# Attention into a mixture of experts on one core: the spread of the input scale gets a buffer of its own width, and the second layer's halves, sums and readings follow a new table of steps

## The chip, the core and the metric

The program runs on one core of one Trainium2 chip. The core has four compute engines, each with an instruction queue that it works off in order: TensorE (PE, matrix products into the accumulators called PSUM), VectorE (DVE), ScalarE (ACT) and GpSimd (POOL). Almost all transfers between the chip's main memory and the core's working memory are issued by a fifth queue, SyncE (SP). An instruction waits at the head of its queue for semaphores that others raise. The metric is the device time of one execution in microseconds (us), from the first to the last instruction plus a small margin, as the median of several runs.

## The reference, cut to what matters

Attention over clusters gives x, 3,072 rows of 512. Then comes a dense mixture of 8 experts: every expert works on every row, and a gate that is normalised eight times in both directions weighs the results.

```python
h = np.maximum(x @ w1[e], 0.0)        # 3072x512 @ 512x1024, for e in range(8)
ye = h @ w2[e]                        # 3072x1024 @ 1024x512
out += P[:, e:e + 1] * ye
```

All of it is float32. The kernel gets that precision out of 16-bit products: each operand is split into a "hi" half (the value rounded to 16 bits) and a "lo" half (what the rounding left), and three products hi·hi, hi·lo, lo·hi are summed.

## The kernel before, in words

**Stages.** The 3,072 rows are four batches b of 768. The first stage is the attention for all batches; each batch of x is stored to main memory (`xd`). The second stage does both layers of all eight experts for batch 0 and prepares the first-layer weights for the rest: 32 blocks t (eight experts, four quarters f2 of the 1,024 hidden columns each). The third stage does batches 1 to 3: 24 slots n, one for each pair (b, e) of batch and expert.

**Seven products instead of eight.** Both layers use Strassen's scheme on 2 by 2 blocks, in the variant with running sums: sums and differences of blocks (S1 to S4 of the left operand, T1 to T4 of the right) are formed first, and seven products replace eight. In the third stage a slot is cut into 28 steps (`SLOT`). In each step the program emits one of the 28 first-layer products of slot n (`layer1b`, seven m = 0..6 for each of the four f2; six matmuls at L1125 each) and a quarter of one of the seven second-layer products of slot n-1 (`layer2b`, nine matmuls at L1532). So the second layer of a slot runs one slot later than its first layer. In the planner's tables, `base` is the first step of the slot in which a slot's second layer runs.

**What feeds the second layer.** The first layer's results are the blocks B11, B12, B21, B22 of each of two row groups g (g = 0 from f2 = 0 and 1, g = 1 from f2 = 2 and 3). POOL forms the differences T1 to T4 of these (`minus`, L1433). Then ACT writes the hi half of each operand (`high`, L1438), and DVE the lo half (`low`, L1442), into tiles called `ho`. The product of operand i of the list ORDER2 (B11, T1, T2, B21, T3, B22, T4) takes the steps base+4i to base+4i+3: two for g = 0, two for g = 1. At the end of each product DVE adds it, weighed by the gate, to the running results (`evict`, L1508): six instructions for the first product, three for each later one. The left operands `w2o` are loaded eight steps ahead (`load_left`, L1446) into three buffers.

**What the first layer needs of the other engines.** A PSUM tile of layer 1 is read by ACT (L1148, L1571) or by DVE's "add" (L1139) before PE may use that buffer again; there are two buffers, so the product m = 6 waits for the add of m = 4.

**The second layer's weights.** In the eight slots of batch 1 the S blocks of the second matrix are made as well, one f2 after the other: SP loads a block into `r` (L1450, two buffers of pool `rp`), POOL forms four sums in `s2w` (`second_sums`, four instructions at L1181, one buffer of pool `sp`), ACT and DVE make their halves `w2s` (`second_high` L1459, `second_low` L1463), and SP stores them to `w2d` (L1466), from which `load_left` reads.

**The next batch's input.** `next_x` (L1089) is a generator that is stepped once in a block of the second stage and four times in a slot of the third. It loads x of the next batch in four blocks, takes the largest absolute value of each, forms differences (`less`, on POOL, L301), and writes the halves of seven operands. In between stands `spread_powers` (L1065). It finds the largest value over all 128 partitions: `am` (one number for each partition) is stored to a small tile in main memory (`amx`, L1068) and read back so that every partition gets all 128 numbers (`all`, L1070). The same function serves the weights with n = 2 numbers a partition (`amw`). Its tile is 128 by 2 numbers wide whatever n is, so that for n = 1 every second number of a row is filled.

**Who sets the order.** In the second and third stage each engine's order is the order in which the program is written: `at(time, ...)` files a small task under a step, and at each step the program emits the layer-1 product, the leftovers of the step before, the tasks of this step, a step of `next_x` (at every seventh), and the layer-2 quarter. So a row of `plan_slot` (L1471) decides where in an engine's queue an instruction stands. SP's queue is in the same order: a load that has to wait holds back the loads behind it.

Of the kernel before, what the change touches and what calls it, by code (L numbers as in the profile page):

```python
# [8 lines left out]
F32 = mybir.dt.float32  # L9
# [5 lines left out]
ALU = mybir.AluOpType  # L15
AX = mybir.AxisListType.X
# [4 lines left out]
P = 128  # L21
# [135 lines left out]
def attn_moe_kernel(  # L157
# [11 lines left out]
    nc = tc.nc  # L169
# [35 lines left out]
    first = const.tile([2, 1], F32, name="first")  # L205
# [62 lines left out]
    def input_use(b, g, pool):  # L268

        nc.vector.tensor_copy(gx[:, b : b + 1], g)  # L270
        inv = pool.tile([P, 1], F32, name="xinv")
        nc.vector.tensor_scalar(out=inv, in0=g, scalar1=1.0 / MX, scalar2=None, op0=ALU.mult)
        nc.vector.reciprocal(sx[:, b : b + 1], inv)
# [16 lines left out]
    def largest(out_, in_):  # L290
        nc.vector.tensor_reduce(out=out_, in_=in_, axis=AX, op=ALU.max, apply_absolute_value=True)
# [7 lines left out]
    def less(o, a, c, by=nc.vector):  # L299
        t = tmp.tile([P, KC, HB], F32, name="tx")  # L300
        by.tensor_tensor(out=t, in0=xq[a], in1=xq[c], op=ALU.subtract)  # L301
        xq[o] = t

    def split_hi(b, o):
        nc.scalar.activation(xs[b][o][:, 0], xq[o], AF.Copy, scale=sx[:, b : b + 1])

    def split_lo(b, o):
        nc.vector.scalar_tensor_tensor(
            out=xs[b][o][:, 1].rearrange("p c s -> p (c s)"), in0=xq[o].rearrange("p c s -> p (c s)"), scalar=sx[:, b : b + 1],
            in1=xs[b][o][:, 0].rearrange("p c s -> p (c s)"), op0=ALU.mult, op1=ALU.subtract,  # L310
        )

    with ExitStack() as actx:
# [48 lines left out]
        bufs = {nm: [] for nm in NSET}  # L362
# [644 lines left out]
    NP2 = NF // 2  # L1007
# [8 lines left out]
    def pool(name, bufs, under=ctx, **kw):  # L1016
        return under.enter_context(tc.tile_pool(name=name, bufs=bufs, reuse_waits="tile", **kw))
# [8 lines left out]
    gs = pool("gs", 2)  # L1026
# [38 lines left out]
    def spread_powers(am, n, name, use):  # L1065

        d = dram.tile([P, n], F32, name=name)
        nc.sync.dma_start(out=d, in_=am)  # L1068
        t = gs.tile([P, P, 2], F32, name="all")
        nc.sync.dma_start(out=t[:, :, 0:n], in_=d.partition_broadcast(P))  # L1070
        yield
        yield
        yield
        g = gs.tile([P, 2], F32, name="gmax2")
        nc.vector.tensor_reduce(out=g[:, 0:n], in_=t[:, :, 0:n].rearrange("p q n -> p n q"), axis=AX, op=ALU.max)
        nc.vector.tensor_scalar(out=g[:, 0:n], in0=g[:, 0:n], scalar1=float(2.0**-100), scalar2=None, op0=ALU.max)
        nc.vector.tensor_single_scalar(out=g[:, 0:n].bitcast(I32), in_=g[:, 0:n].bitcast(I32), scalar=0x7F800000, op=ALU.bitwise_and)
        use(g[:, 0:n])
        yield
# [9 lines left out]
    def next_x(b):  # L1089

        am4 = gs.tile([P, 4], F32, name="am4")
        for i, o in enumerate(XQ):
            k, j = divmod(i, 2)
            xq[o] = pers.tile([P, KC, HB], F32, name=f"xq{o}", tag=xq_from[o][1])
            nc.sync.dma_start(out=xq[o], in_=xd[b][:, k * KC : (k + 1) * KC, j * HB : (j + 1) * HB])
        yield
        for i, o in enumerate(XQ):
            largest(am4[:, i : i + 1], xq[o].rearrange("p c s -> p (c s)"))
            yield
        for t, a, c in LESS["T2"]:  # L1100
            less(t, a, c, nc.gpsimd)
        am = gs.tile([P, 1], F32, name="am")
        nc.vector.tensor_reduce(out=am, in_=am4, axis=AX, op=ALU.max)
        yield from spread_powers(am, 1, f"amx{b}", lambda g: input_use(b, g, gs))
        yield
        for o in XS:
            if o == "B21":
                for t, a, c in LESS[o]:
                    less(t, a, c, nc.gpsimd)
            xs[b][o] = xp.tile([P, 2, KC, HB], F16, name="xst")  # L1110
            split_hi(b, o)
            split_lo(b, o)
            nc.sync.dma_start(out=xsd[b][o], in_=xs[b][o].rearrange("p x c s -> p (x c s)"))
            yield
# [80 lines left out]
    with ExitStack() as ax:  # L1195
# [17 lines left out]
        def scan(idx):  # L1213

            e, f2 = divmod(idx, NP2)
            if f2 == 0:
                ams[e] = gs.tile([P, 2, NP2], F32, name="am8")
            for m in range(2):
                largest(ams[e][:, m, f2 : f2 + 1], raws[idx][:, m * 1024 : (m + 1) * 1024])
                yield  # L1220
            if f2 == NP2 - 1:
                am2 = gs.tile([P, 2], F32, name="am2")
                nc.vector.tensor_reduce(out=am2, in_=ams[e], axis=AX, op=ALU.max)
                yield from spread_powers(am2, 2, f"amw{e}", lambda g: weight_use(e, g, gs))
# [113 lines left out]
        for t in range(NI):  # L1338
            e, f2 = divmod(t, NP2)
# [11 lines left out]
            if t == 8:  # L1351
                inputs = next_x(1)
# [57 lines left out]
        plan.keep_order()  # L1410

    rp = pool("rp", 2)
    sp = pool("sp", 1)
    w2p = pool("w2p", 2)
    hbp = pool("hbp", 3)
    hop = pool("hop", 6)
# [5 lines left out]
    SLOT = 7 * NP2  # L1422
    tasks = {}

    def at(time, f, *a):
        tasks.setdefault(time, []).append((f, a))
# [44 lines left out]
    def plan_slot(n):  # L1471

        b, e = slots[n]
        base = SLOT * (n + 1)
        for g, (t1, t2, t3, t4), off in ((0, (-4, -3, -2, 8), -6), (1, (1, 2, 3, 11), -3)):
            at(base + t1, minus, n, g, "T1", "B12", "B11", "B11")
            at(base + t2, minus, n, g, "T2", "B22", "T1", None)
            at(base + t3, minus, n, g, "T3", "B22", "B12", "B12")
            at(base + t4, minus, n, g, "T4", "B21", "T2", "B21")
            for i, (_, o) in enumerate(ORDER2):  # L1480
                late = 1 if g and o == "T1" else 0
                at(base + 4 * i + off + late, high, n, g, o)
                at(base + 4 * i + off + late + 1, low, n, g, o)
        for i in range(7):
            at(base + 4 * i - 8, load_left, n, i)
        at(base - 1, gate_slot, n)
        if b == 1:
            for f2 in range(NP2):
                t0 = base - SLOT + 6 * f2
                at(max(t0 - 4, 0), load_second, e, f2)  # L1490
                at(t0 + 1, second_sums, e, f2)
                at(t0 + 3, second_high, e, f2)
                at(t0 + 4, second_low, e, f2)

    CHAINS = ("pa", "pc", "pb", "pa", "pb", "pc", "pb")
    INTO = ((("C21", 0), ("X", 1)), (("C22", 1),), (("C12", 1),), (("C11", 0),), (("C22", 1),), (("C12", 1),), (("C21", 0),))
# [83 lines left out]
    for n in range(NS):  # L1580
        plan_slot(n)
    inputs = iter(())
    for n in range(NS + 1):
        one = layer1b(n) if n < NS else iter(())
        two = layer2b(n - 1) if n else iter(())
        if n < NS:
            b, e = slots[n]
            if e == 1 and b + 1 < B:
                inputs = next_x(b + 1)
        for s in range(SLOT):  # L1590
            now = SLOT * n + s
            old = rests[:]
            rests.clear()
            step(one)
            for f in old:
                f()
            for f, a in tasks.pop(now, ()):
                f(*a)
            if s % 7 == 5:
                step(inputs)  # L1600
            step(two)
            plan.keep_order()
# [24 lines left out]
```

## Time and profile before

| | us |
|---|---|
| median of 3 runs | 2664.49 |
| the runs | 2663.87, 2664.49, 2674.68 |
| the profiled execution, its own time | 2661.44 |
| its span, first to last instruction | 2659.7 |
| PE busy in the span | 2305.4 (87%) |
| DVE, ACT, POOL busy | 1711.6, 1038.4, 1097.9 |
| mean granted TensorE clock | 0.937 |

The profile is of one execution. In its timelines a row gives start, length, engine, line, operation, what is written and read, how many such in a row, and in brackets how long the engine was idle just before and who ended that wait. "SPq" is SP issuing a transfer: its length is how long the issue held the queue, not how long the transfer took. In the chain of waits (the work that ended last, followed back) a row is start, length and what. A block of the second stage takes 14.60 us when nothing is in the way, a slot of the third 55.27 us, and so a step of a slot 1.97 us.

### The profile page before, as it was taken

The numbers are of one execution on the slowest core, as the hardware profiler recorded it, in microseconds if no ns is written. First come the engines' busy times: TensorE is split into PE (matmuls) and PEld (weight loads), VectorE is DVE, ScalarE is ACT, GpSimd is POOL, SyncE is SP. The second block draws the span as 40 slices with busy tenths as digits, with TensorE's granted clock in tenths as the row PEclk, the third lists the DMA queues.
The fourth block names the chain that finished last, engine by engine and source line by source line (L and its number), as shares of the span: only waits on it lengthen the run. The fifth ranks groups of instructions, "written<-read, shape, count | busy, mean of one in ns | idle before, by whom it ended". The sixth has DMA issues, their size and how long they took to land.

```text
span 2659.7 us, 39413 instructions
## 1 busy us (share of the span) xinstructions
PE 2305.4 (87%) x15410; PEld 1529.2 (57%) x15410; DVE 1711.6 (64%) x2834; ACT 1038.4 (39%) x1849; POOL 1097.9 (41%) x1007
## 2 busy tenths in 40 slices
PE   7999999879961999899069999992499999999998
PEld 4565565435530545467047777771377777777777
DVE  7888888687841776477047776661266656666667
ACT  4565555534430444343024444331143333333333
POOL 5676777535440455254045455230132233223223
PEclk7999999889985999999579999996799999999999
DMA  7444655264613552574156656530354354444343
GB/s 150 105 117 92 146 130 140 69 227 145 196 31 87 167 169 97 182 260 143 1 185 221 218 198 230 189 120 1 103 164 151 127 175 157 141 133 133 128 134 95
DMA packets 261740, 376.14 MB, mean 141 GB/s; under 512 B 114864, under 2 KB 190768, under 8 KB 261040
## 3 DMA queue, kind: packets, MB, share of 16 engines
q1 hardware_dynamic: 261552, 373.61, 46.1%
q8 instruction: 121, 1.98, 0.3%
q14 instruction: 67, 0.55, 0.1%
HBM read 265.27 MB, written 79.57 MB: 130 GB/s over the span
## 4 chain that ended last, share of the span: by engine, by line
PE 71%; DVE 12%; SPq 6%; another core or an unknown queue 3%; DMA 3%; POOL 2%; issue 2%; ACT 1%; DVEq 0%; ACTq 0%; POOLq 0%
PE h_ps L1125 29%; PE pb L1532 10%; PE pa L1532 6%; PE pc L1532 5%; SPq L1086 5%; PE av_ps L825 4%; PE o_ps L1305 3%; PE o_ps L1304 3%; PE o_ps L1306 3%; PE max_ps L698 2%; PE exp_ps L766 2%; DVE ho L1442 2%; PE exp_ps L767 2%; DVE mrt L702 2%
## 5 line engine op out<-in xcount | busy, mean ns | idle before, releaser
L1125 PEld LDWEIGHTS <-wa 128*128 128x128 f16 x5376 | 529.2, 99 | 454.6 <-issue 157.4
L1532 PEld LDWEIGHTS <-ho 128*128 128x128 f16 x6048 | 593.5, 98 | 309.2 <-issue 169.3
L1125 PE MATMUL h_ps<-xsT,wa 128*128 128x384 f16 x3072 | 591.3, 329 | 103.5 <-DVE u L1139 78.5
L1532 PE MATMUL pb<-w2o,ho 128*128 128x256 f16 x2592 | 331.4, 274 | 167.6 <-DMA w2o<-w2d 167.1
L1125 PE MATMUL h_ps<-xsB,wa 128*128 128x384 f16 x2304 | 440.7, 328 | 35.0 <-DVE B L1139 33.0
L1433 POOL TENSOR_TENSOR B<-B,B 128x768 f32<-128x768 f32 x96 | 181.4, 1890 | 602.4 <-DVE ho L1442 417.1
L1573 ACT ACTIVATE B<-B 128x384 f32<-128x384 f32 x288 | 149.6, 520 | 516.9 <-DVE B L1139 516.9
L1139 DVE SCALAR_TENSOR_TENSOR u<-h_ps,m 128x384 f32<-128x384 f32 x256 | 141.6, 553 | 325.6 <-PE h_ps L1125 322.5
L1442 DVE TENSOR_TENSOR ho<-B,ho 128x768 f16<-128x768 f32 x288 | 326.1, 1138 | 14.2 <-ACT ho L1438 14.2
L792 POOL TENSOR_TENSOR psum<-psum,pe 128x512 f32<-128x512 f32 (+1 forms) x203 | 221.8, 1110 | 46.1 <-ACT pe L773 40.3
L1438 ACT CAST ho<-B 128x768 f16<-128x768 f32 x288 | 231.6, 824 | 12.4 <-POOL B L1433 7.2
L1532 PE MATMUL pc<-w2o,ho 128*128 128x256 f16 x1728 | 220.5, 274 | 1.3 <-DVE ho L1442 1.3
L1532 PE MATMUL pa<-w2o,ho 128*128 128x256 f16 x1728 | 219.0, 273 | 0.0
L702 DVE TENSOR_REDUCE mrt<-max_ps 128x1 f32<-128x512 f32 (+1 forms) x288 | 189.9, 683 | 38.4 <-PE max_ps L698 36.6
L1139 DVE SCALAR_TENSOR_TENSOR B<-h_ps,u 128x384 f32<-128x384 f32 x192 | 106.0, 552 | 164.6 <-PE h_ps L1125 163.6
L773 ACT ACTIVATE pe<-exp_ps 128x512 f32<-128x512 f32 x288 | 165.9, 597 | 82.7 <-PE exp_ps L767 76.4
L1433 POOL TENSOR_TENSOR B<-B,T 128x768 f32<-128x768 f32 x48 | 95.3, 1987 | 216.6 <-DVE ho L1442 216.6
L1366 ACT ACTIVATE hh<-c 128x384 f16<-128x384 f32 x128 | 67.0, 523 | 220.8 <-DVE c L1139 219.6
L1304 PE MATMUL o_ps<-wb,hh 128*128 128x512 f16 x384 | 147.6, 384 | 0.0
L1305 PE MATMUL o_ps<-wb,hh 128*128 128x512 f16 x384 | 147.5, 384 | 0.0
L1306 PE MATMUL o_ps<-wb,hl 128*128 128x512 f16 x384 | 147.3, 384 | 0.0
L1181 POOL TENSOR_TENSOR s2w<-r 128x256 f32<-128x256 f32 x64 | 55.9, 873 | 204.3 <-DMA r<-in_moe_w 132.0
(235 smaller groups left out, 3265.0 us busy)
## 6 DMA issues: line engine op xcount, KB each, us to landing
wa<-w1d SPq DMA_DIRECT2D x96, 896.0 KB
w2o<-w2d SPq DMA_DIRECT2D x168, 512.0 KB
raw<-in_moe_w SPq DMA_DIRECT2D x64, 512.0 KB
w1d<-wa SPq DMA_DIRECT2D x32, 896.0 KB
r<-in_moe_w SPq DMA_DIRECT2D x32, 512.0 KB
w2d<-w2s SPq DMA_DIRECT2D x32, 512.0 KB
w2d<-wb SPq DMA_DIRECT2D x96, 128.0 KB
qn<-in_q SPq DMA_DIRECT2D x16, 384.0 KB
```

The costliest lines, as they stand in the source:

```text
L702: nc.vector.tensor_reduce(out=t["mr"][:, i0 : i0 + ni, ni - 1], in_=ps.rearrange("p (x c) -> p x c", x=ni), axis=AX, op=ALU.max)
L773: nc.scalar.activation(pe, ps.rearrange("p (x c) -> p x c", x=ni), AF.Exp, scale=SCALE)
L792: (nc.gpsimd if e == POOL else nc.vector).tensor_tensor(out=st[:, a:z], in0=old[a], in1=part, op=ALU.add)
L1125: nc.tensor.matmul(ps[:, 0:HB], wa[:, w_, a, c, :], x[:, x_, c, :], start=(first and s_ == 0), stop=(s_ == len(steps) - 1), skip_group_che ...
L1139: nc.vector.scalar_tensor_tensor(out=t, in0=ps[:, 0:HB], scalar=KAPPA, in1=x, op0=ALU.mult, op1=ALU.add)
L1304: nc.tensor.matmul(po[i], hh[:, t, ti], wbh[:, t], start=(first and t == 0), stop=False)
L1305: nc.tensor.matmul(po[i], hh[:, t, ti], wbl[:, t], start=False, stop=False)
L1306: nc.tensor.matmul(po[i], hl[:, t, ti], wbh[:, t], start=False, stop=(last and t == 1))
L1433: nc.gpsimd.tensor_tensor(out=t, in0=d[a], in1=d[c], op=ALU.subtract)
L1438: nc.scalar.copy(t[:, 0], blocks[n, g][o])
L1442: nc.vector.tensor_tensor(out=t[:, 1], in0=blocks[n, g][o], in1=t[:, 0], op=ALU.subtract)
L1532: nc.tensor.matmul(ps[:, q], h[:, h_, f, q * P : (q + 1) * P], w[:, 2 * g + f, w_], start=(first and g == 0 and s_ == 0 and q % 2 == 0), s ...
```

## The change

It has four parts. (1) In `spread_powers` the tile that receives the spread numbers is now exactly n wide, with its own name for each n and one buffer. (2) In `next_x` a `yield` follows each `less`, so that the four differences fall in four calls instead of two; everything behind them in `next_x`, the store of `amx` included, comes two calls later, and from the fifth operand on four calls later. (3) In `plan_slot` the steps of `minus`, `high` and `low` change: the differences of g = 0 come one step later; the hi half of T1 (g = 0 and 1) and T2 (g = 0) comes one step later; the lo halves of g = 0 come two steps behind the hi half (T1: one), and those of T1 (g = 1) and T2 (g = 0) go from step 3 to steps 4 and 5. (4) The four blocks of second-layer weights in a slot of batch 1 change their steps: sums at -5, 5, 9, 13 of the slot, hi at 0, 8, 12, 16, lo and store at 1, 9, 13, 17 (before: sums 1, 7, 13, 19; hi 3, 9, 15, 21; lo 4, 10, 16, 22), in the first slot at 3, 7, 11, 15 and so on; the loads follow; `s2w` has two buffers instead of one.

```diff
@@ spread_powers
-        t = gs.tile([P, P, 2], F32, name="all")
-        nc.sync.dma_start(out=t[:, :, 0:n], in_=d.partition_broadcast(P))
+        t = gs.tile([P, P, n], F32, name=f"all{n}", bufs=1)
+        nc.sync.dma_start(out=t, in_=d.partition_broadcast(P))
...
-        nc.vector.tensor_reduce(out=g[:, 0:n], in_=t[:, :, 0:n].rearrange("p q n -> p n q"), axis=AX, op=ALU.max)
+        nc.vector.tensor_reduce(out=g[:, 0:n], in_=t.rearrange("p q n -> p n q"), axis=AX, op=ALU.max)
@@ next_x
         for t, a, c in LESS["T2"]:
             less(t, a, c, nc.gpsimd)
+            yield
...
             if o == "B21":
                 for t, a, c in LESS[o]:
                     less(t, a, c, nc.gpsimd)
+                    yield
@@
-    sp = pool("sp", 1)
+    sp = pool("sp", 2)
@@ plan_slot
-        for g, (t1, t2, t3, t4), off in ((0, (-4, -3, -2, 8), -6), (1, (1, 2, 3, 11), -3)):
+        for g, (t1, t2, t3, t4) in enumerate(((-3, -2, -1, 9), (1, 2, 3, 11))):
...
-                late = 1 if g and o == "T1" else 0
-                at(base + 4 * i + off + late, high, n, g, o)
-                at(base + 4 * i + off + late + 1, low, n, g, o)
+                h = {("T1", 0): -1, ("T1", 1): 3, ("T2", 0): 3}.get((o, g), 4 * i - (3 if g else 6))
+                at(base + h, high, n, g, o)
+                at(base + {("T1", 1): 4, ("T2", 0): 5}.get((o, g), 4 * i - (2 if g else 4)), low, n, g, o)
...
-            for f2 in range(NP2):
-                t0 = base - SLOT + 6 * f2
-                at(max(t0 - 4, 0), load_second, e, f2)
-                at(t0 + 1, second_sums, e, f2)
-                at(t0 + 3, second_high, e, f2)
-                at(t0 + 4, second_low, e, f2)
+            first = base - SLOT
+            times = ((3, 7, 11, 15), (8, 12, 16, 20)) if n == 0 else ((-5, 5, 9, 13), (1, 9, 13, 17))
+            for f2, (t0, t1) in enumerate(zip(*times)):
+                at(first + (t0 - 6 if f2 < 2 else times[0][f2 - 2] + 1) if n else (0 if f2 < 2 else times[0][f2 - 2] + 1), load_second, e, f2)
+                at(first + t0, second_sums, e, f2)
+                at(first + t1 - 1, second_high, e, f2)
+                at(first + t1, second_low, e, f2)
```

DVE at the start of slot 3 (batch 1), before. `u` and `B` are the layer-1 adds, `ho` the lo halves (of T2 with g = 0 and of T1 with g = 1, which lies in the tile B), `C` and `X` the first of the six evictions of the first product:

```order
L1139 SCALAR_TENSOR_TENSOR u_12512<-h_ps,m_12490 128x384
L1139 SCALAR_TENSOR_TENSOR u_12560<-h_ps,m_12490 128x384
L1442 TENSOR_TENSOR ho<-T_12424,ho 128x768
L1442 TENSOR_TENSOR ho<-B_12224,ho 128x768
L1508 SCALAR_TENSOR_TENSOR C_11190<-pa,gates,C_11190 128x256
L1508 SCALAR_TENSOR_TENSOR X<-pa,gates,X 128x256
...
L1139 SCALAR_TENSOR_TENSOR B_12589<-h_ps,u_12560 128x384
L1463 SCALAR_TENSOR_TENSOR w2s<-s2w,s_97,w2s 128x4x256
```

The same place after (lines are two or three higher in the changed file); the first `ho` is that of T1 with g = 0, the last two are T1 with g = 1 and T2 with g = 0:

```order
L1444 TENSOR_TENSOR ho<-B_11893,ho 128x768
L1141 SCALAR_TENSOR_TENSOR u_12523<-h_ps,m_12498 128x384
L1465 SCALAR_TENSOR_TENSOR w2s<-s2w,s_97,w2s 128x4x256
L1141 SCALAR_TENSOR_TENSOR u_12562<-h_ps,m_12498 128x384
L1511 SCALAR_TENSOR_TENSOR C_11201<-pa,gates,C_11201 128x256
L1511 SCALAR_TENSOR_TENSOR X<-pa,gates,X 128x256
...
L1141 SCALAR_TENSOR_TENSOR B_12591<-h_ps,u_12562 128x384
L1444 TENSOR_TENSOR ho<-B_12222,ho 128x768
L1141 SCALAR_TENSOR_TENSOR B_12612<-h_ps,m_12498 128x384
L1444 TENSOR_TENSOR ho<-T_12444,ho 128x768
```

The two lo halves that stood between the adds and the evictions now stand behind the evictions and behind the add `B` that PE's product m = 6 waits for; one lo half and one `w2s` stand ahead of them instead.

SP around the spread for batch 2, before (in slot 2, at step 12):

```order
L1446 DMA w2o<-w2d_6150 128x2048
L1068 DMA amx_12131<-am 128x1
L1070 DMA all<-amx_12131 128x128x1
L1086 DMA wa<-w1d_6129 128x3584
L1450 DMA r_12183<-in_moe_w 128x2x512
L1446 DMA w2o<-w2d_6150 128x2048
```

After (in slot 2, at step 26):

```order
L1452 DMA r_12405<-in_moe_w 128x2x512
L1068 DMA amx_12449<-am 128x1
L1070 DMA all_12451<-amx_12449 128x128
L1452 DMA r_12475<-in_moe_w 128x2x512
L1086 DMA wa<-w1d_6131 128x3584
L1448 DMA w2o<-w2d_6151 128x2048
```

The spread has become a plain 128 by 128 transfer and stands 14 steps later, again ahead of a load of `r`, one of `wa` and one of `w2o`.

## The prediction

> **What bounds the kernel now.** I read the page's slices first.
>
> ```profile
> span 2659.7 us, 39413 instructions
> PE   7999999879961999899069999992499999999998
> PEclk7999999889985999999579999996799999999999
> ```
>
> Each digit is 66.5 us. From the second slice on PE is full nearly everywhere, so PE's work is the floor; but three holes stand out, at slices 12 and 13, 20 and 21, 28 and 29, and the granted clock falls with them (to 5 tenths). The waits view says who ends PE's long waits:
>
> ```profile
> PE pb L1532 <- DMA w2o<-w2d: 167.1, 3, 83.2
> PE h_ps L1125 <- DVE u L1139: 78.5, 2, 78.1
> ```
>
> Two waits of 83 us for a load of `w2o` and one of 78 us behind DVE. What held the loads is in SP's timeline, at the three places (stage two, slot 2, slot 10):
>
> ```profile
> 751.77 0.32 SPq L1068 DMA_DIRECT2D amx<-am  x1
> 759.61 0.37 SPq L1070 DMA_DIRECT2D all<-amx  x1
> 760.04 79.34 SPq L1209 DMA_DIRECT2D raw<-in_moe_w  x1
> 1247.89 0.33 SPq L1068 DMA_DIRECT2D amx<-am  x1
> 1255.36 0.37 SPq L1070 DMA_DIRECT2D all<-amx  x1
> 1255.82 82.78 SPq L1086 DMA_DIRECT2D wa<-w1d  x1
> 1338.69 0.39 SPq L1450 DMA_DIRECT2D r<-in_moe_w  x1
> 1339.17 3.73 SPq L1446 DMA_DIRECT2D w2o<-w2d  x1
> 1791.67 0.32 SPq L1068 DMA_DIRECT2D amx<-am  x1
> 1799.77 0.37 SPq L1070 DMA_DIRECT2D all<-amx  x1
> 1800.23 78.72 SPq L1086 DMA_DIRECT2D wa<-w1d  x1
> ```
>
> Each time the issue right behind `all<-amx` takes 79 to 83 us, whatever it loads, where others take 0.4. The spread itself clogs the queue: 128 by 128 numbers into every second place are 16,384 pieces of 4 bytes. The same spread for the weights, twice the bytes but without holes, is one row of the chain, and the chain also gives the lengths of stages:
>
> ```profile
> 579.47 5.15 DMA all<-amw
> 606.86 1.95 PE h_ps L1125 x12
> 621.46 1.95 PE h_ps L1125 x12
> 738.22 1.95 PE h_ps L1125 x12
> 864.57 1.95 PE h_ps L1125 x12
> 1094.16 1.95 PE h_ps L1125 x12
> 1230.64 2.08 PE h_ps L1125 x6
> 1666.19 1.14 PE h_ps L1125 x6
> 1916.76 1.14 PE h_ps L1125 x6
> 2580.02 1.14 PE h_ps L1125 x6
> ```
>
> 5.15 us instead of 79. The first rows stand at the same place of their blocks: a block is 621.46 - 606.86 = 14.60 us. The last four stand at the m = 6 product of the first quarter of slots 2, 8, 11 and 23: the last twelve slots take (2580.02 - 1916.76)/12 = 55.27 each. PE's own timeline has a wait at that product in every slot:
>
> ```profile
> 1131.40 2.08 PE L1125 MATMUL h_ps<-xsB,wa 128*128 128x384 f16 x6 [8.05 <-DVE B L1139]
> 1171.00 1.14 PE L1125 MATMUL h_ps<-xsB,wa 128*128 128x384 f16 x6 [2.46 <-DVE B L1139]
> 1350.71 2.08 PE L1532 MATMUL pb<-w2o,ho 128*128 128x256 f16 x9 [82.14 <-DMA w2o<-w2d]
> 1377.89 1.14 PE L1125 MATMUL h_ps<-xsB,wa 128*128 128x384 f16 x6 [2.88 <-DVE B L1139]
> 2027.31 1.14 PE L1125 MATMUL h_ps<-xsB,wa 128*128 128x384 f16 x6 [0.30 <-DVE B L1139]
> 2630.65 1.92 PE L1532 MATMUL pc<-w2o,ho 128*128 128x256 f16 x16 [1.30 <-DVE ho L1442]
> ```
>
> It is 0.30 us in a slot of batches 2 and 3 (2027.31) and 2.88 in a slot of batch 1 (1377.89). Why there, DVE and POOL show around 1372; the third row of DVE is the quiet slot.
>
> ```profile
> 1370.15 0.56 DVE L1139 SCALAR_TENSOR_TENSOR u<-h_ps,m 128x384 f32<-128x384 f32 x1 [3.28 <-PE h_ps L1125]
> 1370.62 1.91 DVE L1442 TENSOR_TENSOR ho<-T,ho 128x768 f16<-128x768 f32 x1
> 1372.45 2.56 DVE L1442 TENSOR_TENSOR ho<-B,ho 128x768 f16<-128x768 f32 x1
> 1377.76 1.27 DVE L1463 SCALAR_TENSOR_TENSOR w2s<-s2w,s,w2s 128x1024 f16<-128x1024 f32 x1
> 2022.62 0.95 DVE L1442 TENSOR_TENSOR ho<-T,ho 128x768 f16<-128x768 f32 x1
> 1369.88 1.83 POOL L1433 TENSOR_TENSOR T<-B,B 128x768 f32<-128x768 f32 x1
> 1371.66 2.55 POOL L1433 TENSOR_TENSOR B<-B,B 128x768 f32<-128x768 f32 x1
> ```
>
> Beside POOL's subtractions the two lo halves take 1.91 + 2.56 = 4.47 us, alone 2 x 0.95. The difference, 2.57, is all of 2.88 - 0.30: the four sums for the second layer push POOL's differences on until they meet the lo halves, and both stand ahead of the add that PE waits for.
>
> **The change part by part.** The sum is made on the profiled execution: 2661.44 us, of which the span is 2659.7. Its rows give the stretches.
>
> (1) The spread. Now 128 rows of 512 bytes, half of `all<-amw`: I take its 5.15 us as the upper bound, nothing as the lower, and 5 as the value. It is hidden: in stage two the raw weights are loaded blocks ahead, in stage three `w2o` eight steps, 8 x 1.97 = 15.8 us. From 738.22 to 864.57 are three blocks and 126.35 us: 126.35 - 43.8 = 82.5 too many. I leave 1.5 of it (two differences on POOL still fall here): **-81**. Slots 2 to 8 are 1666.19 - 1230.64 = 435.55 for six slots, six at 55.27 are 331.6: 103.9 too many, 82.14 of them the stall, the rest the waits of 2.88 and PE's slow restart (2.08 us for nine matmuls at 1350.71). Slots 8 to 11 are 250.57, three at 55.27 are 165.8: 84.8 too many.
>
> What stays is the store of `amx`. SP waits for its landing before it can issue `all`: 7.84, 7.47 and 8.10 us between the first two rows of each place. Before it stood behind a `w2o` load at step 12, now at step 26, two steps ahead of a slot. Queued behind it are `all`, `r`, `wa` and a `w2o` that PE wants eight steps after its step. If the store goes out two steps after its own, as before, that `w2o` is issued about 7.8 + 3 x 0.4 = 9 us late and has 15.8 - 9 = 6.8 us to land behind them. Bounds: 0, and the 1350.71 - 1339.17 = 11.5 us that PE waited from the issue of a `w2o` in a full queue, less 6.8, so 4.7. I take **+1**, near the lower end, since the 11.5 hold the tail of the 4-byte pieces; in slot 10 there is no `r` and I take 0.
>
> (2) The yields. From 864.57 to 1094.16 are 15 blocks and 229.59 us, 10.6 above 15 x 14.60; that is where the differences and splits of batch 1's input run. Two differences in one call become one in each of two. The work stays, only its lump is cut: gain between 0 and 10.6, I take **-3**. In stage three the whole of `next_x` ends five slots after its start instead of four, still before the slot that reads it.
>
> (3) The steps of the halves. Of the two lo halves that stand ahead of the evictions none is left there, so DVE can start them 1.9 us sooner and the 0.30 goes. T1 for g = 1 is now ready only after the evictions (six, then the add, then 0.95): some 0.7 us before PE reads it, by the rows of slot 11. Between 0 and 0.30 a slot; I take 55.0. For the fifteen slots from 8 on: 1916.76 - 1666.19 + 663.26 = 913.83 against 15 x 55.0 = 825: **-88.8** (84.8 of it the third stall). At the very end no layer 1 runs between, so a step takes half as long and the lo half of T1, g = 0, one step later, meets PE: the 1.30 at 2630.65 grows by up to 1.6 (a lo half beside POOL), **+1**.
>
> (4) The sums. They leave the steps 1 to 4. What stands ahead of the evictions instead, one lo half (0.95 to 2.56) and one `w2s` (1.27 to, at the same ratio, 3.4), finds DVE idle: 3.28 us before the add at 1370.15 and more before that. So the evictions are not late by more than 6.0 - 3.28 = 2.7, nor early below nothing; I take 0, as `w2s` took 1.27 wherever I saw it. A slot of batch 1 then takes 55.3. Six from 1230.64 on: 435.55 - 331.8 = **-103.7**. Slot 1, from 1171.00 to 1230.64, 59.64 to 55.3: **-4.3**. From 1094.16 to 1171.00 lie the first sums; PE waits 8.05 us there because the first `w2s` stands at step 4 and its load has not landed; at step 8 it costs about 3, and the 2.46 goes: **-7**. Its bounds are 0 and -12.7, all waits there.
>
> The Trainium skill, *SBUF — State Buffer*, section "Who interferes with whom", says that a VectorE instruction with two inputs in SBUF and a GpSimd one that reads it exclude each other for whole instructions. The 2.56 against 0.95 beside a POOL row of 1.83 agree with it. It speaks against spreading POOL's sums over the slot, where each finds a lo half to block; what that would cost is the first rival.
>
> Sum: -81 + 1 - 3 - 88.8 + 1 - 103.7 - 4.3 - 7 = -285.8, so 2661.44 - 285.8 = 2375.6. The median of the runs, 2664.49, lies 3.05 above the profiled execution: **2378 us**.
>
> **The rivals.** *The collisions move along.* The sums now stand at steps 5, 9, 13 and -5, beside the lo halves of T2, B21 and T3. If each slot of batch 1 keeps its 2.6 (seven: 18) and the later differences of g = 0, which now run until the slot starts, cost each of fifteen further slots 2.6 as well (39), the time is 2378 + 57 = 2435. For it: 1372.45. Against: the lo halves there have four steps' room, and PE reads none of them within 2 us.
>
> *The queue behind the store.* The 8 us landing and the loads behind it become the next stall, at the upper bound of 4.7 in slot 3, as much in slot 11 and in stage two: 2378 + 13 = 2391, inside the range.
>
> *The spread stays in pieces.* If the new transfer is still cut into single numbers, two stalls of 82 and one of 79 stay: 2378 + 243 = 2621. Against it: `all<-amw`, 5.15, is shaped alike.
>
> *Slower than before.* A load of `r` that waits for sums which stand behind it in POOL's order holds SP, and `w2o` behind it, in each of the eight slots of batch 1. The order of loads is now 0, 2, 1, 3 with two buffers, so the load at step 6 must get the buffer that step 5 frees. If it got the one of step 13, SP would stand for 7 x 1.97 = 14 us, less the eight steps of lead, plus the 11.5 of a full queue: some 10 a slot, 80 in all. It decides only from 286/8 = 36 us a slot on; nothing in the trace reaches that. At 40 a slot: 2378 + 320 = 2698.
>
> **How the numbers follow.** My forecast with its bounds 0.85, the collisions 0.08, the queue 0.04 (inside the range too), the pieces 0.02, slower 0.01. The range: all that I left (1.5, 7.6, 3, 1, 1, and 0.3 in seven slots) gone is 16 less, 2362. Upward, the seven slots of batch 1 at their old price are 19 and the late `w2o` 5 more, 2402. About what a measurement of this kernel can tell from no change is 0.5%, 13 us. The forecast, the queue, the collisions and, at 2621, the pieces as well lie below 2651: faster 0.98; within 0.5% 0.01; slower 0.01.
>
> **What would show it.** Right: slices 12, 20 and 28 of PE full, the clock near 1 throughout from the second stage on, the issue behind `all` back to 0.4 us, the packets under 512 bytes down by 49,152, slots of 55.0 to 55.3 from slot 2 on. Wrong: a row of PE with a wait above 2 us that names `w2o` in slot 3, DVE `B` at m = 6 or `ho`, in every slot; a `w2s` or `ho` above 2 us ahead of the evictions.

## The result, and the profile after

| | us | ratio to before, 95% interval |
|---|---|---|
| before, median of 4 runs beside it | 2669.55 (2663.87 to 2674.68) | |
| changed, median of 4 runs | **2372.84** (2370.12 to 2379.8) | 0.8893 (0.8862 to 0.8924) |
| changed, profiled execution | 2373.4, span 2371.3 | |

The forecast was 2378 (2362 to 2402). The page of the changed kernel, to be read against the same rows of before:

```profile
span 2371.3 us, 39383 instructions
PE   7999999987999999999999999999999999999998
PEclk7999999988999999999999999999999999999999
DMA packets 212971, 376.13 MB, mean 159 GB/s; under 512 B 65712, under 2 KB 142000, under 8 KB 212272
```

The three holes of PE are gone and the granted clock has no dips from the second stage on. The page of the kernel before has this line of packets:

```profile
DMA packets 261740, 376.14 MB, mean 141 GB/s; under 512 B 114864, under 2 KB 190768, under 8 KB 261040
```

It counts 114,864 packets under 512 bytes; 65,712 are left, 49,152 fewer, which is 3 x 16,384: each spread had indeed been cut into its single numbers. The Trainium skill, *DMA: Bandwidth & Descriptors*, section "Why a DMA increments its semaphore by 16 and not by 1", says that one descriptor moves one contiguous run of the last dimension. The count agrees to the packet.

SP's timeline of the changed kernel at the spread of slot 2:

```profile
1178.30 0.32 SPq L1068 DMA_DIRECT2D amx<-am  x1
1185.56 0.32 SPq L1070 DMA_DIRECT2D all<-amx  x1
1185.97 0.39 SPq L1452 DMA_DIRECT2D r<-in_moe_w  x1
1186.41 0.46 SPq L1086 DMA_DIRECT2D wa<-w1d  x1
1186.96 1.63 SPq L1448 DMA_DIRECT2D w2o<-w2d  x1
```

The issue behind `all<-amx` takes 0.39 us where it took 82.78. What is left is the 7.26 us from `amx` to `all`, and 1.4 us later a `w2o`. What that costs is in PE's timeline; its other rows are the m = 6 products of the first quarter of slots 1, 2, 8 and 23, and one of the tail:

```profile
1080.76 1.14 PE L1127 MATMUL h_ps<-xsB,wa 128*128 128x384 f16 x6
1135.57 1.14 PE L1127 MATMUL h_ps<-xsB,wa 128*128 128x384 f16 x6
1197.88 1.14 PE L1535 MATMUL pb<-w2o,ho 128*128 128x256 f16 x9 [2.45 <-DMA w2o<-w2d]
1467.82 1.14 PE L1127 MATMUL h_ps<-xsB,wa 128*128 128x384 f16 x6
1638.57 1.14 PE L1535 MATMUL pb<-w2o,ho 128*128 128x256 f16 x9 [0.96 <-DMA w2o<-w2d]
2292.31 1.14 PE L1127 MATMUL h_ps<-xsB,wa 128*128 128x384 f16 x6
2343.53 1.92 PE L1535 MATMUL pc<-w2o,ho 128*128 128x256 f16 x16 [1.87 <-DVE ho L1444]
```

No m = 6 row of these carries a bracket any more: nothing is waited for there. From 1080.76 to 1135.57 a slot of batch 1 takes 54.81 us, the same as most slots of batches 2 and 3. The chain of the changed kernel gives the second stage, blocks 13, 16 and 31:

```profile
739.50 1.95 PE h_ps L1127 x12
785.48 1.95 PE h_ps L1127 x12
1014.49 1.95 PE h_ps L1127 x12
```

With the rows of before that stand at the same places, the difference of the two spans (2659.7 - 2371.3 = 288.4) comes apart like this:

| stretch | before | after | difference | forecast |
|---|---|---|---|---|
| start to block 13 | 738.22 | 739.50 | +1.3 | 0 |
| blocks 13 to 15 | 126.35 | 45.98 | -80.4 | -81 |
| blocks 16 to 30 | 229.59 | 229.01 | -0.6 | -3 |
| block 31 to m = 6 of slot 1 | 76.84 | 66.27 | -10.6 | -7 |
| from there to slot 2 | 59.64 | 54.81 | -4.8 | -4.3 |
| slots 2 to 7 | 435.55 | 332.25 | -103.3 | -103.7 + 1 |
| slots 8 to 22 | 913.83 | 824.49 | -89.3 | -88.8 |
| rest | 79.68 | 78.99 | -0.7 | +1 |

### The profile page after: what moved, and what is told of

Read it like the earlier page. It is cut to its first block, busy times and chain, and to the rows that moved or that the text cites. A ratio compares the mean times of both kernels' runs of the same rounds, so it can differ in the third digit from the quotient of the medians.

```text
span 2371.3 us, 39383 instructions
## 1 busy us (share of the span) xinstructions
PE 2292.8 (97%) x15410; PEld 1525.9 (64%) x15410; DVE 1768.7 (75%) x2834; ACT 1040.8 (44%) x1849; POOL 1139.6 (48%) x1007
## 2 busy tenths in 40 slices
DMA packets 212971, 376.13 MB, mean 159 GB/s; under 512 B 65712, under 2 KB 142000, under 8 KB 212272
## 4 chain that ended last, share of the span: by engine, by line
PE 83%; DVE 9%; DMA 3%; POOL 2%; issue 1%; ACT 1%; SPq 1%; DVEq 0%; ACTq 0%; POOLq 0%
PE h_ps L1127 34%; PE pb L1535 12%; PE pa L1535 8%; PE pc L1535 7%; PE av_ps L825 4%; PE o_ps L1307 3%; PE o_ps L1308 3%; PE o_ps L1306 3%; PE max_ps L698 3%; PE exp_ps L766 3%; PE exp_ps L767 2%; DVE mrt L702 2%; DVE vsum L508 1%; DVE wb L1241 1%; DMA w2o<-w2d 1%
## 5 line engine op out<-in xcount | busy, mean ns | idle before, releaser
L1435 POOL TENSOR_TENSOR B<-B,B 128x768 f32<-128x768 f32 x96 | 198.2, 2066 | 472.4 <-DVE ho L1444 452.0
L1444 DVE TENSOR_TENSOR ho<-B,ho 128x768 f16<-128x768 f32 x288 | 353.3, 1228 | 0.9 <-ACT ho L1440 0.9
L1150 ACT ACTIVATE m<-h_ps 128x384 f32<-128x384 f32 x128 | 62.6, 489 | 202.1 <-PE h_ps L1127 202.0
L1183 POOL TENSOR_TENSOR s1w<-raw 128x256 f32<-128x256 f32 x62 | 45.7, 736 | 206.0 <-ACT raw L1274 206.0
```

The source lines that it names most:

```text
L1435: nc.gpsimd.tensor_tensor(out=t, in0=d[a], in1=d[c], op=ALU.subtract)
L1444: nc.vector.tensor_tensor(out=t[:, 1], in0=blocks[n, g][o], in1=t[:, 0], op=ALU.subtract)
```

## The experiments

Eleven runs in three batches; those of one batch share a chip and the runs of the kernel before. The medians of before were 2657.55 (7 runs) beside the first four, 2660.64 (7) beside the next four and 2661.89 (9) beside the last three, and 2669.55 in the result. So a difference under some 12 us between batches is read from rows, not from medians.

**The theory** was that of the prediction: the 16,384 pieces stop SP three times for 79 to 83 us, and the rest, some 45 us, is lo halves that stand ahead of an add PE waits for and are held up by POOL. **Rivals**: the parts overlap, so that one of them alone brings nearly all, or the steps cure something other than contention.

### The spread alone

The kernel before, with part (1) only:

```diff
-        t = gs.tile([P, P, 2], F32, name="all")
-        nc.sync.dma_start(out=t[:, :, 0:n], in_=d.partition_broadcast(P))
+        t = gs.tile([P, P, n], F32, name=f"all{n}", bufs=1)
+        nc.sync.dma_start(out=t, in_=d.partition_broadcast(P))
...
```

> Part 1 alone: the buffer of its own width, no yields, the old steps and sums. Theory (the three long stalls are the 4-byte pieces alone, and nothing else rests on them): the block or slot in which each stall lay goes to its neighbours' length, so the profiled span falls by 80.9 + 89.2 + 84.8 = 255, from 2659.7 to about 2405; slots of batch 1 stay at 58, later ones at 55.27. Rival (the stalls also gave the other engines time to catch up, and the new table is what lets the queues keep pace): PE waits of over 2 us for POOL or DVE appear in the blocks and slots where a stall was, and the span stays above 2425.

Measured: 2413.61 us, ratio 0.9078 (0.9062 to 0.9094), span 2414.1. The stalls are gone; the largest wait of PE that is left is for DVE's add:

```profile
PE h_ps L1125 <- DVE B L1139: 33.1, 26, 7.6
```

Of the 288.4 us this part alone brings 2659.7 - 2414.1 = 245.6. That is 9 us less than the theory had: slot 2 takes 63.56 instead of 58, and slots 1 and 3 are some 2 above 58 each. In all three the granted clock falls behind PE's wait for the add: it is 0.73 from 1091.67 to 1098, 0.55 from 1151.3 to 1158 and 0.72 from 1214.8 to 1221, and 1.00 from 1274.5 to 1280, behind the same wait of slot 4. Some 2.7 us more are lost at the end of slot 2. POOL's and PE's rows there:

```profile
1187.42 1.54 POOL L1181 TENSOR_TENSOR s2w<-r 128x256 f32<-128x256 f32 x1 [11.22 <-DMA r<-in_moe_w]
1193.47 1.14 PE L1125 MATMUL h_ps<-xsT,wa 128*128 128x384 f16 x6 [1.74 <-ACT B L1571]
```

The load of `r` went out at 1177.85, behind the store of `amx` (1170.08) and its reading (1176.96). POOL's sums waited for it, ACT's `w2s` for the sums, and the reading of PSUM that PE waited for stands behind that `w2s`. So by the rows this is the queue behind the store; no run separates it. New waits in a slot that held a stall are what the rival named, but they are below its 2 us, and the span is below its 2425.

### The table alone

The kernel before with parts (3) and (4), the spread in pieces.

```diff
-        for g, (t1, t2, t3, t4), off in ((0, (-4, -3, -2, 8), -6), (1, (1, 2, 3, 11), -3)):
+        for g, (t1, t2, t3, t4) in enumerate(((-3, -2, -1, 9), (1, 2, 3, 11))):
...
+            times = ((3, 7, 11, 15), (8, 12, 16, 20)) if n == 0 else ((-5, 5, 9, 13), (1, 9, 13, 17))
```

> Parts 3 and 4 alone: the new steps and sums, the old spread in 4-byte pieces, no yields. Theory: the three stalls of 78 to 84 us stay; the slots of batch 1 go to 55, the first slot to 32, the later ones to 54.8; together 35 to 40 us less, span 2620 to 2625. Rival (the new steps only take up time that the stalls had spoilt): span within 5 us of 2659.7.

Measured: 2616.51 us, ratio 0.9838 (0.982 to 0.9856), span 2615.8. PE's waits in this kernel:

```profile
PE pb L1533 <- DMA w2o<-w2d: 161.7, 2, 81.0
PE h_ps L1125 <- DVE u L1139: 77.2, 2, 76.8
```

All three stalls stay, and most slots without one are at 54.81 (slot 4 is the longest, 57.10). This part alone brings 43.9 us, more than the 35 to 40 expected. In the medians of this batch the two parts bring 243.9 and 41.0, in sum 284.9; the next run, which has parts (1), (3) and (4) together, brings 285.5. The two add up, neither hides the other.

### Without the yields

The changed kernel without part (2).

```diff
             less(t, a, c, nc.gpsimd)
-            yield
...
                     less(t, a, c, nc.gpsimd)
-                    yield
```

> The changed kernel without part 2, the yields behind the differences. The prediction gave the yields 3 us: span 2374. What the two traces now suggest (10.0 us too many in the late blocks with the yields, 10.6 without; 2.2 against 1.7 in blocks 14 and 15): no difference, span 2370 to 2373. The spread stands at step 12 of its slot then; the load of w2o behind it is as late as at step 26, so a PE wait of 1 to 3 us for w2o is expected in one slot, whichever.

Measured: 2372.08 us, ratio 0.8919 (0.8901 to 0.8936), span 2368.1. No difference, as expected, but not because the yields do nothing. The blocks first: before and here, seven blocks (19 to 25) are longer, one of them by 5 us; with the yields it is nine blocks, none by more than 1.8. In sum 10.6 us too many in seven became 10.0 in nine. The other expectation was a miss: a late `w2o` of 1 to 3 us was to remain, and there is none; here the store stands at other steps, and the `w2o` behind it goes out 12.02 us after the `w2o` ahead of it, where the changed kernel has 15.96. In the third stage two effects balance. Counted from its first product, slot 4 takes 57.10 us here and slot 12 55.78, with waits for the add `B` (1.29 at most), where the changed kernel has 54.89 and 54.81. With the yields slots 3 and 11 take 57.42 and 55.93, with the waits for `w2o`, where this kernel has 54.81.

### Half as many pieces

The changed kernel with a spread of 128 by 64 pieces of 8 bytes with holes between; the largest value is then taken in two steps.

```diff
-        t = gs.tile([P, P, n], F32, name=f"all{n}", bufs=1)
-        nc.sync.dma_start(out=t, in_=d.partition_broadcast(P))
+        t = gs.tile([P, P, n], F32, name=f"all{n}", bufs=1) if n == 2 else gs.tile([P, P // 2, 4], F32, name="all1", bufs=1)
...
+            nc.sync.dma_start(out=t[:, :, 0:2], in_=d.rearrange("(a b) n -> a (b n)", b=2).partition_broadcast(P))
...
```

> The changed kernel, but the spread of the input scale goes into a buffer in which two of every four numbers are filled: 8,192 pieces of 8 bytes for the same 64 KB. Theory (the price is by the piece): the issue behind it takes about half of 79 to 83 us, 40, and PE stalls 37 to 42 us at each of the three places: span 2485 to 2500. Rival (the price is by the bytes, or a fixed one of any transfer with holes): a stall of about 80 at each place, span about 2615; or none, if 8 bytes are enough, span 2371.

Measured: 2492.93 us, ratio 0.9379 (0.9362 to 0.9396). The packets of the page, then the issue behind the spread in SP's timeline and the wait in PE's:

```profile
DMA packets 237163, 376.13 MB, mean 151 GB/s; under 512 B 90288, under 2 KB 166192, under 8 KB 236464
```

```profile
1218.99 0.37 SPq L1073 DMA_DIRECT2D all<-amx  x1
1219.45 35.51 SPq L1459 DMA_DIRECT2D r<-in_moe_w  x1
```

```profile
1271.24 1.01 PE L1542 MATMUL pb<-w2o,ho 128*128 128x256 f16 x4 [41.77 <-DMA w2o<-w2d]
```

90,288 - 65,712 = 24,576 = 3 x 8,192 packets more, and 41.77 us of wait where it was 82.14; at the other two places PE waits 33.43 and 42.73 us where it waited 78.11 and 83.24. The bytes are the same, and half the pieces cost about half: the price goes by the pieces, 82.78 / 16,384 = 5.1 ns and 35.51 / 8,192 = 4.3 ns each. Why the smaller count costs less by the piece is not shown. The buffer has its own name and one copy here too, so it is not those that took the stalls away.

### The old sums, then the old steps

The changed kernel with part (4) undone, and then with part (3) undone:

```diff
-    sp = pool("sp", 2)
+    sp = pool("sp", 1)
...
+                at(t0 + 1, second_sums, e, f2)
+                at(t0 + 3, second_high, e, f2)
+                at(t0 + 4, second_low, e, f2)
```

> The changed kernel with part 4 undone: the second-layer sums at their old steps 1, 7, 13, 19 with one buffer; the new steps of the halves stay. Theory (the 2.6 us of a batch-1 slot were two lo halves beside POOL, ahead of the evictions): with the halves behind the evictions they are gone although POOL's sums are back at step 1; slots 2 to 7 take 54.8 to 55.5. The first slot is back near 39, since w2s stands at step 4 again. Span 2378 to 2384. Rival (the sums' place in the queue itself makes PE wait): slots 2 to 7 take 57 to 58, span 2390 or more.

Measured: 2382.26 us, ratio 0.896 (0.8943 to 0.8978). The total is as expected, the slots not all. Counted from a slot's first product, as in the next run too, four of the six from slot 2 on take 54.81 to 55.81, but slot 5 takes 58.78 and slot 6 takes 56.80. DVE, POOL and PE in slot 5 of this kernel:

```profile
1305.02 1.88 DVE L1444 TENSOR_TENSOR ho<-B,ho 128x768 f16<-128x768 f32 x1
1306.82 2.82 DVE L1465 SCALAR_TENSOR_TENSOR w2s<-s2w,s,w2s 128x1024 f16<-128x1024 f32 x1
1309.57 0.54 DVE L1141 SCALAR_TENSOR_TENSOR B<-h_ps,m 128x384 f32<-128x384 f32 x1
```

```profile
1306.04 2.52 POOL L301 TENSOR_TENSOR tx<-xqB,xqB 128x768 f32<-128x768 f32 x1
```

```profile
1310.16 1.32 PE L1127 MATMUL h_ps<-xsB,wa 128*128 128x384 f16 x6 [2.14 <-DVE B L1141]
```

A difference of `next_x` on POOL started at 1306.04, `w2s` on DVE at 1306.82, and `w2s` took 2.82 us instead of 1.27. The add behind it came late, and PE waited 2.14.

The steps of the halves as before:

```diff
-        for g, (t1, t2, t3, t4) in enumerate(((-3, -2, -1, 9), (1, 2, 3, 11))):
+        for g, (t1, t2, t3, t4), off in ((0, (-4, -3, -2, 8), -6), (1, (1, 2, 3, 11), -3)):
...
+                late = 1 if g and o == "T1" else 0
+                at(base + 4 * i + off + late, high, n, g, o)
+                at(base + 4 * i + off + late + 1, low, n, g, o)
```

> The changed kernel with part 3 undone: the old steps of the differences and halves, the new sums. Theory: POOL has no sums at step 1, so its differences do not meet the two lo halves that again stand ahead of the evictions, and only the 0.30 us of each slot is back; slots of batch 1 and later take 55.1 to 55.3, the first slot 32; span 2371 + 22 x 0.4 = 2380. Rival (the place of the lo halves alone made the wait, whatever POOL does): slots of batch 1 stay at 57 to 58, span 2395 or more.

Measured: 2394.51 us, ratio 0.9005 (0.8985 to 0.9026), span 2391.8. That is 11.8 above the theory and 3.2 below the rival. Slots from 8 on, all but slot 13, take 55.27 with the wait of 0.30, as the theory says; but five of the six from slot 2 on take 56.63 to 56.65 instead of 55.3, and slot 1 takes 63.89, with a wait of 4.1 for the same add. Slot 4 of this kernel, DVE, POOL and PE:

```profile
1246.30 1.36 DVE L1465 SCALAR_TENSOR_TENSOR w2s<-s2w,s,w2s 128x1024 f16<-128x1024 f32 x1
1250.14 1.78 DVE L1444 TENSOR_TENSOR ho<-T,ho 128x768 f16<-128x768 f32 x1
1251.84 1.48 DVE L1444 TENSOR_TENSOR ho<-B,ho 128x768 f16<-128x768 f32 x1
```

```profile
1246.66 2.67 POOL L1435 TENSOR_TENSOR T<-B,B 128x768 f32<-128x768 f32 x1
1249.30 1.80 POOL L1435 TENSOR_TENSOR B<-B,B 128x768 f32<-128x768 f32 x1
1251.07 1.43 POOL L1183 TENSOR_TENSOR s2w<-r 128x256 f32<-128x256 f32 x1
```

```profile
1256.19 1.14 PE L1127 MATMUL h_ps<-xsB,wa 128*128 128x384 f16 x6 [1.67 <-DVE B L1141]
```

The two lo halves take 1.78 + 1.48 = 3.26 us, 1.36 more than 2 x 0.95, and 1.67 is 0.30 + 1.37. So the wait is again exactly what the lo halves are longer, but the sums of step 1 are not needed for it: the `w2s` that the new table puts there starts 0.36 us ahead of POOL's second difference and stretches it to 2.67, the third then runs to 1251.10, beside the first lo half, and the sums of step 5 stand beside the second.

The two runs show both sides of one rule. Here DVE's `w2s` came first (1246.30 against 1246.66) and POOL's instruction grew; in the run with the old sums POOL's came first (1306.04 against 1306.82) and `w2s` grew. The Trainium skill, *SBUF — State Buffer*, section "Who interferes with whom", says: "Issue order, not op shape, decides who blocks." The rows agree.

### The read one call later

The changed kernel with one more yield between the store of `amx` and its reading, for the input only, so that SP issues other loads while the store lands.

```diff
+        if n == 1:
+            yield
         t = gs.tile([P, P, n], F32, name=f"all{n}", bufs=1)
```

> The changed kernel, with one more yield between the store of amx and the transfer that spreads it (for the input scale alone): seven steps or a block, 13.7 us, lie between, more than the 7.3 to 8.1 us that the store takes to land. Theory: SP no longer stands still, and PE's waits for w2o in slots 3 and 11 (2.45 and 0.96 us) go; span 2367 to 2369, less than the runs scatter. Rival (the transfers themselves crowd the queue, not the wait ahead of them): the waits stay within 1 us of what they were.

Measured: 2368.06 us, ratio 0.8906 (0.8889 to 0.8923). SP's timeline of this kernel:

```profile
1176.21 0.32 SPq L1068 DMA_DIRECT2D amx<-am  x1
1177.58 0.42 SPq L1450 DMA_DIRECT2D w2o<-w2d  x1
1186.75 0.38 SPq L1072 DMA_DIRECT2D all<-amx  x1
```

The `w2o` goes out 1.4 us behind the store instead of 8.7, and slots 3 and 11 take 54.81 each, with no wait. So the waits of 2.45 and 0.96 were the store's landing. The medians can't show 3.4 us; the rows do.

### The input's step at the start of a block, too

In the second stage, on top of that, `next_x` is stepped right behind a block's first product of layer 1 instead of the sixth.

```diff
-                if m == 5:
+                if m == 0:
                     step(inputs)
```

> As the one before, and in stage two the call of next_x moves from product m = 5 to m = 0 of a block, where POOL was idle for 6.7 us. Theory (the late blocks are 10 us too long because a difference on POOL stands ahead of the weights' halves and blocks DVE's wb there, 2.61 us instead of 0.74): blocks 14, 15 and 21 to 29 go from 15.3 - 16.4 to 14.6 - 15.0; span 2356 to 2362. Rival (it is the extra work of ACT and DVE that makes the blocks long, wherever it stands): no change, span 2367 to 2371.

Measured: 2360.33 us, ratio 0.8879 (0.8861 to 0.8897). In the changed kernel the longer blocks end like this (DVE, then PE). POOL runs a difference at 917.82 and, pushed on by it, an instruction for the weights at 919.78, beside this `wb`:

```profile
919.97 2.61 DVE L1241 SCALAR_TENSOR_TENSOR wb<-raw,s,wb 128x512 f16<-128x512 f32 x1
```

```profile
923.76 1.14 PE L1127 MATMUL h_ps<-xsT,wa 128*128 128x384 f16 x6 [1.60 <-DVE c L1141]
```

In this version a `wb` beside a difference on POOL (900.39, 2.13 us) stands early in its block:

```profile
900.77 2.29 DVE L1243 SCALAR_TENSOR_TENSOR wb<-raw,s,wb 128x512 f16<-128x512 f32 x1
```

It still takes 2.29 us where `wb` takes 0.74 alone, but no add is behind it that PE wants soon. Blocks 16 to 30 have 1.6 us too many instead of 10.

### The three beside one another

The changed kernel again, the last version again, and the last version without the yields of part (2), on one chip.

> The changed kernel once more, unaltered, so that the two versions built on it stand beside it on one chip. Every theory expects what it took: a ratio of 0.886 to 0.892 to the kernel before, and in PE's timeline the two waits for w2o at the start of slots 3 and 11, together 3.4 us.

> The version with the spread read one call later and the input's step ahead of a block's first product instead of its sixth, on the same chip as the changed kernel. By the sums of the rows: 3.4 us for the waits behind the store, 9.5 us in the second stage (blocks 13 to 15: 45.99 to 44.9; blocks 16 to 30: 229.0 to 220.6), less 1.3 in slot 1: 11 to 12 us under the changed kernel. If the differences of the medians so far were only those of chips, the two are within 4 us of each other.

> The same version without the yields behind the differences (part 2 undone on top of it). The step now stands where nothing on DVE is waited for within a few us. Theory: splitting the lump of two differences gives nothing by itself, so this is within 3 us of the version with the yields. Rival: the yields do help once the step stands at the right place, since two differences in a row (3.6 us of POOL) reach the next add; then it is 4 us or more slower, with one block of 16 us or more where two differences fall together.

| | median us | ratio, 95% interval |
|---|---|---|
| changed kernel | 2369.28 | 0.8907 (0.8895 to 0.8919) |
| read later, step at the start | 2358.49 | 0.8865 (0.8853 to 0.8877) |
| the same without the yields | 2371.45 | 0.8916 (0.8904 to 0.8928) |

The changed kernel repeats, its two waits for `w2o` too (2.16 and 0.48). The version built on it is 10.8 us faster (11 to 12 were expected), the intervals apart: it beats both kernels. And the third was a miss for the theory: the yields, with no net worth where the change put them, are worth 13 us there. PE's long waits in the version without them:

```profile
743.69 1.14 PE L1127 MATMUL h_ps<-xsT,wa 128*128 128x384 f16 x6 [1.65 <-DVE u L1141]
764.88 1.44 PE L1127 MATMUL h_ps<-xsT,wa 128*128 128x384 f16 x4 [6.44 <-DVE u L1141]
886.58 1.45 PE L1127 MATMUL h_ps<-xsT,wa 128*128 128x384 f16 x6 [2.96 <-DVE u L1141]
```

The rival named two differences in a row; at 743.69 and 886.58 that is what stands ahead (POOL's rows there are two differences of 2.13 and 2.14 us, one behind the other, with a `wb` of 2.30 on DVE beside them); at 886.58 reductions to `gmax` and an `xst` of 1.29 us stand between them and the add as well. The largest, 6.44, is something else, in SP's and DVE's rows of that version:

```profile
743.20 0.34 SPq L1068 DMA_DIRECT2D amx<-am  x1
748.56 0.40 SPq L1068 DMA_DIRECT2D amw<-am  x1
756.81 0.33 SPq L1072 DMA_DIRECT2D all<-amw  x1
```

```profile
761.25 0.42 DVE L1077 TENSOR_REDUCE gmax<-all 128x2 f32<-128x256 f32 x1 [6.05 <-DMA all<-amw]
```

Without the yields the store of the input's `amx` falls 5.4 us ahead of the weights' own store, whose reading then waits 8.25 us instead of 3.34 in the changed kernel (747.16 to 750.50), and DVE stands 6.05 us for it. Block 14, which holds that wait, is 7.7 us longer than with the yields (22.61 against 14.90), blocks 13 and 22, which hold the others, 1.1 and 4.1. So more than half of what the yields are worth there is the place of the store, not the splitting of the lump. Why the second store lands later behind the first was not separated.

## Why the prediction was right, point by point

**The stall** was sized right: the three stretches that held one gave -80.4, -103.3 and -89.3 against -81, -102.7 and -88.8. Reading it as a price by the piece holds (half the pieces, about half the stall), and so does the sum of parts (284.9 against 285.5). The total is nearer than its terms, and that is in part luck: the first slot came out 3.6 us better than forecast and the tail 1.7 better, blocks 16 to 30 2.4 worse and the start 1.3 worse.

**The late `w2o`**, +1, should have been 3.4: 2.45 in slot 3 and 0.96 in slot 11, where I took 0. A wait above 2 us for `w2o` in slot 3 was also one of the signs named for being wrong. The failed step was "near the lower end, since the 11.5 hold the tail of the 4-byte pieces". The chain of the changed kernel has that load from issue to landing:

```profile
1186.96 10.88 DMA w2o<-w2d
```

That is 10.88 us with no 4-byte pieces about; what stands ahead of it are `r` and `wa`. PE wanted it at 1197.88 - 2.45 = 1195.43, so by a lead of 15.8 it was due out at 1179.6; it went out at 1186.96, 7.3 late, with 8.5 us left, and 10.88 - 8.5 is the 2.4.

**The yields**, -3, brought -0.6, and nothing net between the kernels with and without. The failed step is "only its lump is cut: gain": the lump was cut, but nine blocks collide instead of seven, and the input's step stood just ahead of an add that PE waits for. That place was the cost: moved to the start of the block, 8.4 us went.

**The first slot**, -7, brought -10.6. The first part of it, "at step 8 it costs about 3", was right: PE's waits there are now 2.08, 0.36 and 0.40 us, 2.84 in all. But with the 8.05 and the 2.46 the four short waits between them (0.48, 0.77, 0.41 and 0.53) went too, 2.2 us that the forecast does not count.

**The steps and the sums** came out right as a sum, with the split between them wrong. "The difference, 2.57, is all of 2.88 - 0.30: the four sums for the second layer push POOL's differences on until they meet the lo halves" gave all of it to the sums of step 1. With the sums moved and the halves left, 1.36 of the 2.57 is still there; with the halves moved and the sums left, four slots of six are at 54.81 to 55.81. Either edit takes away much of the same wait, which is why the separate prices would have misled while the sum did not. The arithmetic itself, wait = 0.30 + what the lo halves are longer, held in both places where I could test it. "`w2s` took 1.27 wherever I saw it" fell too, in the changed kernel as well. DVE there, ahead of the evictions of slot 2, which begin at 1131.86:

```profile
1126.19 2.42 DVE L1444 TENSOR_TENSOR ho<-B,ho 128x768 f16<-128x768 f32 x1
1129.00 2.37 DVE L1465 SCALAR_TENSOR_TENSOR w2s<-s2w,s,w2s 128x1024 f16<-128x1024 f32 x1
```

The prediction named "a `w2s` or `ho` above 2 us ahead of the evictions" as a sign of being wrong. It came, and PE waited for nothing at m = 6. So the 0 that I took there holds, but not for its reason: the two did grow, inside the bound of 6.0, and DVE still reached the add in time.

**The slot** is 54.81, below the 55.0 and 55.3 I took: the 0.30 went entirely, and 0.16 with it (55.27 - 0.30 - 54.81). **The tail**: +1 was -0.7. The wait for `ho` grew from 1.30 to 1.87, but before there were two more behind it (0.45 and 1.72, the last for a `w2o`), and in their place are two of 0.34.

**The rivals.** The collisions did move along, and grew: a `w2s` takes 1.68 us in the mean where it took 1.28, a lo half 1.20 where it took 1.13. But they are not where PE waits: from slot 2 to the tail, and apart from the two for `w2o`, PE's only waits above 0.2 us are two of 0.45, in slots 6 and 14, where a lo half and an `xst` (1.83 and 2.48 us in slot 6) stand ahead of the add together. The queue behind the store became the largest wait that is left in the slots, at half its price of 4.7 in slot 3, a fifth in slot 11 and none in stage two. Nothing was seen of the pieces. Loads of `r` did hold SP, as the last rival had it: the waits of SP name POOL's sums seven times for them, 27.6 us in all and 6.5 at most, where the kernel before has eight of 3.3 in all. That is below the 10 us a slot of that rival, and PE's two waits for `w2o` went when the store's reading was moved, so no wait of PE in the slots is left as its price.

**Two rows** were misread. The quiet slot in the rows of DVE is the fifth (2022.62), not the third; and the lo half of 2.56 us stands beside POOL's row of 2.55 us, the one of 1.91 beside that of 1.83. Neither enters the sum.

## What to carry to other kernels

Before costing a table of steps, look for an issue that takes tens of us: the transfer just ahead of it is the one to look at, and here its count of pieces, not its bytes, was the price. A store that is read back at once should have other issues put between. When two engines hold each other up, what counts is not whether they collide but whether an instruction that a third engine waits for stands behind: move the pair in front of work with slack, and then try again the edits that brought nothing, since their worth depends on the place.

## What the runs showed of the hardware that was not expected

- A store of one 4-byte number from each of 128 partitions holds the reader that follows it at once for 6.60 to 8.10 us in the kernels here; the same store with 8 bytes a partition took 3.12 us in the chain of the changed kernel, 2.51 to 3.81 in those of the others, and 8.18 us once, 5.4 us behind a store of the first kind.
- Behind 16,384 pieces SP's next issue is held 79 to 83 us whatever it moves, behind 8,192 pieces 34.3 to 35.5 us; the bytes are the same.
- A spread of 64 KB in rows of 512 bytes left the next issue at 0.39 us.
